# Seven block products for eight in the second layer of each chunk pair, and the pairs' instructions in the order of a list schedule

## The chip, the cores and the metric

The kernel runs on one core of a Trainium2 chip. The metric is the device time of one execution in microseconds (us); the median of three runs of the kernel before is 654.4 us (654.15 to 655.77). The engines are named as the profile names them: PE is TensorE with its matmuls, PEld its weight loads, DVE is VectorE, ACT is ScalarE, POOL is GpSimd, and SP issues the transfers.

## What is computed

Two blocks follow each other. The first is a linear recurrence over 768 time steps, for 4 batches and 8 heads of 48 channels; the second is a gated feed-forward block on 3072 tokens of 384 features with 1536 hidden units. All of it is fp32.

```
for t in range(S):                       # attention, per batch and head
    y[t]  = r[t] @ (state + outer(u * k[t], v[t]))
    state = w[:, None] * state + outer(k[t], v[t])
x  = y, heads side by side               # 3072 x 384
xn = x / sqrt(mean(x*x) + 1e-6) * rms_g
out = (silu(xn @ w_gate) * (xn @ w_val)) @ w_out
```

## The kernel before

The 768 steps are cut into 12 chunks of 64, so that one chunk of the 4 batches is 256 tokens. The kernel's own word for the recurrence, the mean of squares and the scaling of one chunk is **mixing**; its result is x, kept twice (`xa`, and `xb` with the two halves of 64 partitions exchanged). Each matmul of the program appears in the profile as two MATMUL records.

**The first stage** (chunks 0 and 1, with the loading and conversion of the weights) is given in an order that a small planner finds. `Plan.add` (line 103) takes each step with its engine, an estimated duration, the keys that it reads and writes, and the closure that issues it; `Plan.schedule` (line 123) is a greedy list schedule in which each engine takes the ready step with the earliest due time; `Plan.run` (line 174) tries 3000 sets of due times and issues the steps in order of their planned starts. Matmuls on a constant (`warm`, line 852) fill the planned gaps of PE up to 25 us.

**The pairs.** Chunks 2 to 11 go through the feed-forward block in five pairs, and here the order is written out by hand (lines 1015 to 1055). For a pair (s, s+1) the first layer has six groups (`group`, line 945). Each group forms gate and value of 128 units of each half of the hidden layer for both chunks by seven products of blocks where the plain way has eight: `first` to `seventh`, each 6 matmuls of 64 rows x 128 by 256 columns, 12 records, into three PSUM tiles a, b, c. The sums that such a scheme needs are made by DVE: of weights once (`unit_sum`), of tokens once for each pair (`token_sum`: t1, t2, x of s+1 in its own place, t4), of products in each group. The hidden values end in six tiles h, with four 256-token parts each.

The second layer is plain. `project` (line 996) is called for j = 0 to 3, each 128 tokens of the pair; it accumulates 12 matmuls of 128 x 128 by 384 columns into one PSUM bank, in two halves of 6 matmuls, then ACT copies the bank to SBUF and SP stores it. The mixing of the next two chunks is written in between: that of s+2 in the groups, that of s+3 between the halves of the projections (the letters in `plan` and in the calls of `mix`). Three places for x go round (`ring`, bufs=3).

**The check of the weights.** While the pairs run, all weights are read from HBM a second time in 48 pieces of 288 words (`check`, line 930) into a tile of their own, and ACT looks at them with an Abs and a Relu that sums; at the end DVE and PE condense the findings to a number `bad`, on which the program branches to a general version (not taken here).

All instructions are recorded through the helper of line 91, so the profile is read by tile names: `a`, `b`, `c` are the first layer, `po` the second, `py`, `pa`, `pu`, `pm` the mixing in the pairs, `first_a` to `first_c` and `at` the first stage.

Of the kernel before, what the change touches and what calls it, by code (L numbers as in the profile page):

```python
# [48 lines left out]
P = 128  # L50
# [43 lines left out]
class Plan:  # L94
# [28 lines left out]
    def schedule(self, goals, free):  # L123
# [16 lines left out]
        for _ in range(n):  # L140
            when, e = min((max(free[e], min(at[i] for i in ready[e])), e) for e in free if ready[e])
            i = min((i for i in ready[e] if at[i] <= when), key=lambda i: late[i])
            sooner = [j for j in ready[e] if at[j] <= when + 0.3 and late[j] < late[i] - 1]
# [30 lines left out]
    def run(self, cells, first, free, idle=None, trials=3000):  # L174

        goals, t = {}, first
        for i in cells:
            goals[i] = t  # L180
            t += self.ops[i][1]
        rng, best = random.Random(3), None
        for trial in range(trials):
            new = dict(goals)
            if trial and rng.random() < 0.5:
                a, by = rng.randrange(len(cells)), rng.uniform(-15, 15)
                for i in cells[a : a + 1 + int(rng.expovariate(1 / 6))]:
                    new[i] += by
            elif trial:
                new[rng.randrange(len(self.ops))] = rng.uniform(0, t)  # L190
            start = self.schedule(new, free)
            end = self.replay(start, free)
            end = max(end[i] for i in cells) + 0.3 * sum(end[i] for i in cells) / len(cells)
            if best is None or end <= best[0]:
                best, goals = (end, start), new
        self.start = best[1]
        busy = free["PE"]
        for i in sorted(range(len(self.ops)), key=lambda i: (self.start[i], i)):
            if self.ops[i][0] == "PE":
                if idle and busy < first:  # L200
                    idle(self.start[i] - busy)
                busy = self.start[i] + self.ops[i][1]
            self.ops[i][3]()
# [3 lines left out]
def fast(ctx, tc, chan, tok, vpad, wka, wkb, wot, cols, u_row, out, bad):  # L207
# [17 lines left out]
    ring = ctx.enter_context(tc.tile_pool(name="ring", bufs=3))  # L225
    hpool = ctx.enter_context(tc.tile_pool(name="hpool", bufs=7))
    ps_gv = ctx.enter_context(tc.tile_pool(name="ps_gv", bufs=1, space=PSUM))
    ps_at = ctx.enter_context(tc.tile_pool(name="ps_at", bufs=2, space=PSUM))
# [52 lines left out]
    gdup = raws.tile([P, HP, 2, L], FP32, name="gdup")  # L281
# [25 lines left out]
    def state_decay():  # L307

        for z in range(2):
            rows = slice(64 * z, 64 * z + D)  # L310
            for p in range(HP):
                act.mul(
                    KH[rows, z, :, p, :], free_dims(ident[rows, 64 * z : 64 * z + D], (0, B), (1, D)),
                    pows[L][rows, p : p + 1],
                )
# [104 lines left out]
    def diagonal(s, half, side):  # L420

        t, rows = SIDES[side]
        for b in (2 * half, 2 * half + 1):
            for p in range(HP):
                x = b * HP + p
                act.mul(t[rows, b, p, :], dmask[rows], du_of[s][rows, x : x + 1])
# [94 lines left out]
    xa, xb = {}, {}  # L521
# [5 lines left out]
    def mean_squares(bank, sq):  # L527
        for half in range(2):
            for i in range(CC):
                pe.matmul(  # L530
                    bank[:, 2 * P + half : 2 * P + half + 1], sq[:, i, half * P : (half + 1) * P], ones[:, 0:1],
                    start=i == 0, stop=i == CC - 1, skip_group_check=True,
                )
# [34 lines left out]

    late = {}

    def begin_sums():
        loading.close()
        mine = late["mine"] = ctx.enter_context(tc.tile_pool(name="mine", bufs=1))
        for n in (1, 2, 4):
            late[f"s{n}"] = [mine.tile([P, NQ, CC, P], FP32, name=f"s{n}_{i}") for i in range(2)]

# [10 lines left out]
    t1, t2, t4 = {}, {}, {}  # L587

    def token_sum(s, n):

        new = lambda t: t.setdefault(s, late["mine"].tile([P, CC, NT], FP32, name=f"t{n}_{s}", tag=f"t{n}"))
        if n == 1:
            dve.tensor_sub(new(t1), xa[s + 1], xa[s])
        elif n == 2:
            dve.tensor_sub(new(t2), xb[s + 1], t1[s])
        elif n == 3:
            dve.tensor_sub(xa[s + 1], xb[s + 1], xa[s + 1])
        else:
            dve.tensor_sub(new(t4), xb[s], t2[s])
# [3 lines left out]
    add = p.add  # L603
    at = [ps_at.tile([P, 512], FP32, name=f"at_{i}", tag="at") for i in range(2)]
    gv = {t: ps_gv.tile([P, 2, 512], FP32, name=f"first_{t}", tag=t) for t in "abc"}
    hbuf = [hpool.tile([P, 4, NT], FP32, name=f"hbuf_{i}", tag="h") for i in range(7)]
    yT = one.tile([P, CC, NT], FP32, name="yT_first", tag="yT")
    sq = one.tile([P, CC, NT], FP32, name="sq_first", tag="sq")
    ms = c_tile([P, 2], "ms")
    diag = one.tile([P, 2, P], FP32, name="diag", tag="rms")  # L610
    turn = {"at": 0, "gv": 0, "h": 0}

    def next_at():
# [3 lines left out]

    add("SP", 0.3, [], ["w"], lambda: None, land=1.9)
    add("DVE", 2.4, ["w"], ["pw"], powers, name="powers")
    add("DVE", 0.43, ["pw"], ["up"], lambda: dve.tensor_mul(up, pw, by_inv), port=True)  # L620
    add("DVE", 0.43, ["pw"], ["down"], lambda: dve.tensor_mul(down, pw_rev, by_inv), port=True)
    add("DVE", 0.22, [], ["dmask"], lambda: dve.tensor_add(dmask, ident[:, 0:64], ident[:, 64:128]), port=True)
    add(
        "DVE", 0.86, ["pw"], ["gdup"], lambda: [
            dve.tensor_mul(gdup[:, :, z, :], pw_rev, free_dims(pows[L // 2], (1, HP), (0, L))) for z in range(2)
        ], port=True,
    )
    bank, key = next_at()
    add("PE", 0.9, ["gdup"], [key], lambda bank=bank: token_powers(bank), name="wk")
    add("ACT", 0.7, [key], ["wk"], lambda bank=bank: keep_token_powers(bank), name="wk")  # L630
    add("ACT", 3.0, ["pw"], ["khd"], state_decay, name="khd")
# [16 lines left out]

    def mixing(s):
        quick = s == 0  # L650
        if quick:
            ku = hbuf[6].rearrange("p a (h t) -> p a h t", h=HP)
            add("ACT", 1.6, ["w", "CHk0", "CHk1"], ["ku"], lambda: u_k(s, ku), name=f"ku {s}")
            for half in range(2):
                add(
                    "PE", 1.05, ["ku", "CHr0", "CHr1"], [f"first{half}"],
                    lambda half=half: products(gv["a"][:, half], half, ku, CH[:, 0], CH[:, 0]), name=f"E {s}",
# [32 lines left out]
        for half in range(2):  # L690
            bank, key = two[half]
            for side in range(2):
                dst = f"M{'EO'[side]}t{half}"
                if quick:
                    add(
                        "DVE", 0.69, [f"first{half}", "dmask"], [dst],
                        lambda half=half, side=side: diagonal_from(gv["a"][:, half], half, side), name=f"d {s}",
                    )
                else:
                    add("ACT", 2.0, ["du"], [dst], lambda half=half, side=side: diagonal(s, half, side), name=f"d {s}")  # L700
# [28 lines left out]
        add("PE", 1.35, ["sq0", "sq1"], [key], lambda bank=bank: mean_squares(bank, sq), name=f"r {s}")  # L729
        add("ACT", 0.3 if s == 0 else 2.9, [key], ["ms"], lambda bank=bank: root(bank, ms), name=f"sqrt {s}")  # L730
        add("DVE", 0.45, [], ["ms", "diag"], lambda: inverse(ms, diag), name=f"inv {s}")
        add("PE", 0.45, ["diag"], [key], lambda bank=bank: spread(bank, diag), name=f"spread {s}")
        x = s % 3

        def scale(bank=bank):
            xa[s] = ring.tile([P, CC, NT], FP32, name=f"xa_{s}", tag="xa")
            xb[s] = ring.tile([P, CC, NT], FP32, name=f"xb_{s}", tag="xb")
            scaled(s, bank, yT)

        add("DVE", 1.0, [key, "yT0", "yT1"], [f"xa{x}"], scale, name=f"x {s}")  # L740
        for z in range(2):
            add("ACT", 0.83, [f"xa{x}"], [f"xb{x}.{z}"], lambda z=z: exchange(s, z), name=f"xb {s}")
        for z in range(2):
# [3 lines left out]
            "PE", 1.9, ["KH0", "KH1", "khd", "VSv", "VSs0", "VSs1"], [last[0][1], last[1][1]],  # L747
            lambda: [states(last[half][0], half) for half in range(2)], name=f"U {s}",
        )
        for half in range(2):  # L750
            bank, key = last[half]
            add("ACT", 1.07, [key], [f"VSs{half}"], lambda bank=bank, half=half: keep_states(bank, half), name=f"E {s}")

# [15 lines left out]
    cells, sums, waiting = [], {}, deque()  # L769

    def next_gv():
        t = "abc"[turn["gv"] % 3]
        turn["gv"] += 1
        return gv[t], ["first0", "first1"] if t == "a" else [f"gv_{t}"]

    def gate_val(s, i, o):
        ps_, keys = next_gv()
        n = turn["h"]
        turn["h"] = (n + 1) % 24
        h, x = hbuf[n // 4][:, n % 4], s % 3  # L780
# [12 lines left out]
    def add_cell(s, i, hs):  # L793

        po, keys = next_gv()
# [9 lines left out]
        if i == 0:  # L805
            sums[s] = work.tile([P, 2, DM], FP32, name=f"o_{s}", tag="o", bufs=FIRST)
            add("ACT", 0.8, keys, [f"o{s}"], lambda: act.copy(sums[s], po[:, :, 0:DM]), name=f"o {s}")
        else:
            add("DVE", 0.96, keys, [f"o{s}"], lambda: dve.tensor_add(sums[s], po[:, :, 0:DM], sums[s]), name=f"o {s}")
        if i == WQ - 1:  # L810
            add("SP", 0.5, [f"o{s}"], [], lambda: [store(sums[s][:, j], s, j) for j in range(2)])
# [19 lines left out]
    add("DVE", 0.0, ["rounded", "up", "down", "wk"], ["sums"], begin_sums)  # L831
# [20 lines left out]
    def warm(us):  # L852

        for _ in range(int((us - 0.3) / 0.22)):
            pe.matmul(gv["c"][:, 0, 0:P], ones, ones, start=True, stop=True)

    p.run(cells, 25.0, {"PE": 1.5, "DVE": 1.5, "ACT": 2.5, "POOL": 6.3, "SP": 1.8}, warm)
# [698 lines left out]
```

## Time and profile before

| stretch | us | PE busy | DVE busy | ACT busy |
|---|---|---|---|---|
| 0 to 60 (first stage) | 60.0 | 54.40 | 48.91 | 42.91 |
| 60 to 155.8 (first stage) | 95.8 | 95.80 | 70.42 | 52.29 |
| pair of chunks 2, 3 | 101.0 | 99.94 | 61.04 | 49.77 |
| pair 4, 5 | 101.1 | 100.92 | 58.68 | 56.57 |
| pair 6, 7 | 101.0 | 100.81 | 58.67 | 56.45 |
| pair 8, 9 | 101.1 | 100.91 | 56.81 | 56.56 |
| pair 10, 11 and the end | 93.1 | 85.85 | 30.14 | 27.30 |

The table is read off the busy times by window, and the bounds of the pairs are the starts of `first` of the first group. A row tells how much of a stretch each engine works; what an engine waits for stands in other views. The profiled execution took 654.79 us, of which the span from the first to the last instruction is 653.1 us. The granted PE clock is 0.996 over the span.

### The profile page before, as it was taken

To read this page: it belongs to the slowest core of one execution; us is meant where nothing else is said; L and a number is where in the kernel's file an instruction comes from. 1 tells how busy PE (TensorE), PEld (TensorE's weight loads), DVE (VectorE), ACT (ScalarE), POOL (GpSimd) and SP (SyncE) were. 2 spreads that over 40 slices of the span, in tenths; PEclk is the share of its full clock that TensorE was granted. 3 is DMA by queue.
4 is the path that set the end of the run, shared out by engine and by line. 5 is a ranking of instruction groups with operands and counts; after the bars stand their busy time and mean duration, and the time that the engine had idled before them with its cause. 6 is when DMAs were issued, how large, how long until landed. Compare 5 with 4: busy or idle time off the path is not lost.

```text
span 653.1 us, 15289 instructions
## 1 busy us (share of the span) xinstructions
PE 638.6 (98%) x6534; PEld 504.7 (77%) x6534; DVE 384.7 (59%) x560; ACT 341.9 (52%) x952; POOL 41.7 (6%) x39
## 2 busy tenths in 40 slices
PE   9889999999999999999999999999999999999996
PEld 8868777787878766889766888866888966788753
DVE  6988878855765734765743576653576562555400
ACT  5695465944364653574672564673555582433400
POOL 3154423100000000000000000000000000000000
PEclk9999999999999999999999999999999999999999
DMA  8786643053004242204331404332312321122211
GB/s 260 254 310 213 194 116 115 12 170 78 27 3 167 61 138 49 75 22 166 98 111 40 110 20 158 93 93 73 93 37 101 106 73 25 42 63 73 55 27 28
DMA packets 20398, 64.50 MB, mean 99 GB/s; under 512 B 2912, under 2 KB 6112, under 8 KB 18912
## 3 DMA queue, kind: packets, MB, share of 16 engines
q1 hardware_dynamic: 20320, 63.42, 32.3%
q8 instruction: 53, 0.87, 0.6%
q14 instruction: 25, 0.20, 0.1%
HBM read 58.69 MB, written 4.72 MB: 97 GB/s over the span
## 4 chain that ended last, share of the span: by engine, by line
PE 86%; DVE 5%; ACT 4%; issue 2%; DMA 1%; POOL 0%; DVEq 0%; ACTq 0%; POOLq 0%; SPq 0%
PE po L91 24%; PE b L91 15%; PE a L91 10%; PE c L91 9%; PE first_c L91 5%; PE first_b L91 5%; PE first_a L91 5%; PE at L91 4%; PE py L91 4%; PE pa L91 2%; PE pu L91 2%; ACT ME L91 1%; DVE TOK L91 1%; ACT MO L91 1%; DVE gv L91 1%
## 5 line engine op out<-in xcount | busy, mean ns | idle before, releaser
L91 PE MATMUL po<-wo,h 128*128 128x384 f32 x480 | 159.8, 489 | 0.8 <-DVE bad L91 0.8
L91 PEld LDWEIGHTS po<-wo,h 128*128 128x128 f32 x480 | 90.0, 190 | 60.2 <-PE pc L91 0.8
L91 DVE TENSOR_TENSOR gv<-b,m 128x512 f32<-128x512 f32 x90 | 62.1, 690 | 84.2 <-PE b L91 83.5
L91 ACT ACTIVATE gv<-gv 128x512 f32<-128x512 f32 (+1 forms) x60 | 31.0, 518 | 52.9 <-DVE gv L91 52.9
L91 DVE TENSOR_TENSOR gv<-c,gv 128x512 f32<-128x512 f32 x60 | 41.4, 690 | 15.0 <-PE c L91 14.0
L91 ACT COPY o<-po 128x384 f32<-128x384 f32 x20 | 9.5, 474 | 77.4 <-PE po L91 39.2
L91 ACT ACTIVATE ME<-dmask,du 64x64 f32<-64x64 f32 x176 | 43.8, 330 | 9.8 <-DVE du L91 9.4
L91 PE MATMUL a<-xa,wa 64*128 64x256 f32 x360 | 45.0, 383 | 0.7 <-DVE h L91 0.7
L91 PE MATMUL b<-xa,wa 64*128 64x256 f32 x360 | 44.4, 379 | 0.6 <-DVE gv L91 0.6
L91 ACT ACTIVATE MO<-dmask,du 64x64 f32<-64x64 f32 x176 | 44.4, 334 | 0.7 <-DVE du L91 0.3
L91 PE MATMUL c<-xb,s 64*128 64x256 f32 x360 | 44.3, 378 | 0.0
L91 PE MATMUL b<-t,wb 64*128 64x256 f32 x360 | 44.3, 378 | 0.0
L91 PE MATMUL b<-t,s 64*128 64x256 f32 x360 | 44.0, 377 | 0.3 <-DVE gv L91 0.3
L91 PE MATMUL a<-xb,wb 64*128 64x256 f32 x360 | 43.9, 376 | 0.0
L91 PE MATMUL c<-t,s 64*128 64x256 f32 x360 | 43.9, 376 | 0.0
L91 PEld LDWEIGHTS a<-xa,wa 64*128 64x128 f32 x360 | 33.8, 187 | 7.2 <-DVE h L91 3.0
L91 PEld LDWEIGHTS b<-xa,wa 64*128 64x128 f32 x360 | 34.2, 187 | 6.1 <-DVE gv L91 2.4
L91 PEld LDWEIGHTS b<-t,s 64*128 64x128 f32 x360 | 34.8, 187 | 4.7 <-DVE gv L91 0.7
L91 PEld LDWEIGHTS a<-xb,wb 64*128 64x128 f32 x360 | 34.9, 187 | 4.0
L91 PEld LDWEIGHTS c<-t,s 64*128 64x128 f32 x360 | 34.9, 187 | 4.0
L91 PEld LDWEIGHTS b<-t,wb 64*128 64x128 f32 x360 | 34.5, 187 | 4.1
L91 PEld LDWEIGHTS c<-xb,s 64*128 64x128 f32 x360 | 34.5, 187 | 4.1
(146 smaller groups left out, 1076.0 us busy)
## 6 DMA issues: line engine op xcount, KB each, us to landing
chan<-in_chan_dram SPq DMA_DIRECT2D x11, 1024.0 KB, 5.0
TOK<-in_tok_dram SPq DMA_DIRECT2D x12, 768.0 KB, 4.6
VS<-in_vpad_dram SPq DMA_DIRECT2D x24, 336.0 KB, 4.8
raw<-in_wot_dram SPq DMA_DIRECT2D x8, 576.0 KB, 5.0
out_dram<-o SPq DMA_DIRECT2D x48, 96.0 KB, 2.2
again<-in_wka_dram SPq DMA_DIRECT2D x16, 288.0 KB, 2.8
again<-in_wkb_dram SPq DMA_DIRECT2D x16, 288.0 KB, 2.8
again<-in_wot_dram SPq DMA_DIRECT2D x16, 288.0 KB, 2.8
```

The source lines that it names most:

```text
L91: return lambda *args, **kwargs: self.tc.keep_in_program_order(give(*args, **kwargs))
```

## The change

It has three parts.

1. **The second layer** (`second_layer`, new). The pair's hidden values form a matrix of 2 x 2 blocks (two chunks by two halves of the hidden units), and the output weights one of 2 x 2 blocks (two halves of the units by two halves of the 384 features). The product is formed by seven products of blocks for eight. Each is 12 matmuls of 128 x 128 by 192 columns. DVE makes four sums of hidden values for each pair (`sum_1` to `sum_4`), five sums of results (u2, u3, c21, c22, c12), and once, in the first pair, eight sums of output weights (`out_sum`); ACT makes two copies.
2. **No new memory for the sums where another stage's tile is free**: sum_1 lies in the tile of gate and value, sum_2 in that of t1 and t2, sum_3 and sum_4 in h itself, the sums of weights in the place of x of chunk 2 (`swap`), the results in the tile of the first stage's results. The checks of weights use `sq`, the squares of the mixing; they are 36 pieces of 384 words instead of 48 of 288, and five of them follow each mixing's use of `sq`. x has two places from the second pair on (`place`).
3. **The order.** The pairs, with mixing, loads and checks, are steps of a second `Plan`. Its due times are those of the products in a row, stretched by 1.19; it is scheduled once, without a search, and a step may be waited for up to 0.5 us if it is more urgent than the ready one. `run` is split into `search` and `give`. In the first stage the estimated durations of some steps are changed, two steps are cut finer, and the first run of `warm` is counted from 0 instead of 1.5 us and shortened by nine matmuls.

```diff
-    def project(s, j, second):
-        ...
-        for m in range(3, 6) if second else range(3):
-            for x in range(2):
-                i, o = divmod(m + x * NN // 2, NQ)
-                at = (j % 2) * P
-                pe.matmul(
-                    po, h_of[s, m][:, 2 * x + j // 2, at : at + P], wo[i][:, o, :],
-                    start=m == 0 and x == 0, stop=m == last and x == 1,
-                )
+    def second_layer(s):
+        bank = {"x": bank_of["a"][:, 0], "w": bank_of["a"][:, 1], "y": bank_of["b"][:, 0], "z": bank_of["c"][:, 0]}
+        keys = {"x": "a0", "w": "a1", "y": "b", "z": "c"}
...
+        def mm(t, reads, left, right, start, name):
+            def give():
+                for j in range(2):
+                    for m in range(NN // 2):
+                        pe.matmul(
+                            flat[t][:, j], left[:, m, j * P : (j + 1) * P], right(*divmod(m, NQ)),
+                            start=start and j == m == 0, stop=m == NN // 2 - 1, skip_group_check=True,
+                        )
+            line.append(add("PE", 3.9, reads, [keys[t]], give, name=f"{name} {s}"))
...
+        add("DVE", 1.66, h_keys[1] + h_keys[3], gs, lambda: dve.tensor_add(sum_1, h[1], h[3]), port=True, name="sum_1")
+        add("DVE", 1.66, h_keys[0] + gs, ts, lambda: dve.tensor_sub(sum_2, sum_1, h[0]), port=True, name="sum_2")
+        add("DVE", 1.66, h_keys[0], h_keys[1], lambda: dve.tensor_sub(h[1], h[0], h[1]), port=True, name="sum_3")
+        mm("x", h_keys[0], h[0], part(0, 0), True, "P1")
+        add("ACT", 0.47, ["a0"], ["m1"], lambda: act.copy(m1, flat["x"]), name="m1")
+        mm("z", gs + out_keys("o1"), sum_1, w2(0), True, "P5")
+        mm("x", h_keys[2], h[2], part(2, 0), False, "P2")
+        add("ACT", 0.47, ["a0"], ["o0"], lambda: act.copy(results[:, 0], flat["x"]), name="c11")
+        result(0, s, 0)
+        add("DVE", 1.66, ts, h_keys[2], lambda: dve.tensor_sub(h[2], h[2], sum_2), port=True, name="sum_4")
+        mm("y", ts + out_keys("o2"), sum_2, w2(1), True, "P6")
+        plus(["o1"], ["b", "m1"], results[:, 1], flat["y"], m1, "u2")
+        mm("y", h_keys[1] + out_keys("o3"), h[1], part(0, 1), False, "P7")
+        plus(["o3"], ["b", "m1"], results[:, 3], flat["y"], m1, "u3")
+        mm("w", h_keys[3] + out_keys("o4"), h[3], w2(2), True, "P4")
+        plus(["o2"], ["a1", "o3"], results[:, 2], flat["w"], results[:, 3], "c21")
+        plus(["o3"], ["c"], results[:, 3], flat["z"], results[:, 3], "c22")
+        mm("z", h_keys[2], h[2], part(2, 1), False, "P3")
+        plus(["o1"], ["c"], results[:, 1], flat["z"], results[:, 1], "c12")
...
+    place = lambda s: s % 3 if s <= FIRST + 1 else (s + 1) % 2
...
+        if until < 27:
+            for _ in range(int((until - since - 0.3) / 0.22) - (9 if since == 0 else 0)):
+                pe.matmul(bank_of["c"][:, 0, 0:P], ones, ones, start=True, stop=True)
...
+        for m in range(NN // 2):
+            group(s, m)
...
+        if s + 2 < NS:
+            mixing(s + 2), loads(s + 3)
+        second_layer(s)
+        if s + 2 < NS:
+            mixing(s + 3)
...
+    free = {"PE": 0.0, "DVE": 0.0, "ACT": 0.0, "POOL": 0.0, "SP": 0.0}
+    p.give(p.schedule(p.goals_of(line, 0.0, 1.19), free, 0.5))
```

## The prediction

> **What bounds the kernel now.** I read the page's first part, then the waits of PE, then the chain that ended last, then the groups by shape.
>
> ```profile
> span 653.1 us, 15289 instructions
> PE 638.6 (98%) x6534; PEld 504.7 (77%) x6534; DVE 384.7 (59%) x560; ACT 341.9 (52%) x952; POOL 41.7 (6%) x39
> ...
> PE 86%; DVE 5%; ACT 4%; issue 2%; DMA 1%; POOL 0%; DVEq 0%; ACTq 0%; POOLq 0%; SPq 0%
> ...
> L91 PE MATMUL po<-wo,h 128*128 128x384 f32 x480 | 159.8, 489 | 0.8 <-DVE bad L91 0.8
> L91 PEld LDWEIGHTS po<-wo,h 128*128 128x128 f32 x480 | 90.0, 190 | 60.2 <-PE pc L91 0.8
> L91 DVE TENSOR_TENSOR gv<-b,m 128x512 f32<-128x512 f32 x90 | 62.1, 690 | 84.2 <-PE b L91 83.5
> ```
>
> PE is busy for 638.6 of 653.1 us, and most of the rest lies outside its work: 6.4 us after its last matmul (copy, store, branch). A busy PE alone could be a PE that stretches its records over waits, so the second view counts: all that PE waited for between its first and last matmul.
>
> ```profile
> PE at L91 <- ACT sq_first L91: 1.7, 1, 1.7
> PE first_c L91 <- DVE pw L91: 1.2, 1, 1.2
> PE first_b L91 <- POOL wa L91: 1.1, 1, 1.1
> PE at L91 <- DVE MO L91: 1.0, 1, 1.0
> PE b L91 <- DVE gv L91: 0.9, 2, 0.6
> PE po L91 <- DVE bad L91: 0.8, 1, 0.8
> PE at L91 <- DVE diag L91: 0.8, 1, 0.8
> PE a L91 <- DVE h L91: 0.7, 4, 0.2
> ```
>
> Columns: total us, times, longest. The sum is 8.2 us, over half of it in the first 45 us; in the pairs PE waits 1.06 us in the first (101.0 less 99.94 busy), about 0.19 us in each of the next three, and 0.8 us for the flag in the last. So in the pairs the time is the sum of PE's instructions, and DVE's largest group has 83.5 us of idle time behind PE. An instruction less on PE is time less, unless the new order makes PE wait.
>
> The third view gives PE's price without overlaps: the chain in order of time, start and us.
>
> ```profile
> 320.27 4.07 PE po L91 x12
> 324.77 3.87 PE po L91 x12
> 328.64 2.01 PE pa L91 x64
> ...
> 349.85 7.74 PE po L91 x24
> 357.59 1.57 PE pu L91 x64
> 359.16 1.50 PE a L91 x12
> ```
>
> Twelve `po` records take 3.87 us: 322.5 ns each[...].
>
> [...]48 records of one column each (`at<-ones,sq_first`) fill 5.9 us, 123 ns each[...], so a load costs no more than that when nothing hides it. [...]The trace has 690 ns for 512 and 1350 for 1152[...]. [...]the stores' pieces shrink from 1536 to 768 B[...]. No run so far shows 768 B.
>
> **The change, part by part.**
>
> *Removed from PE:* 5 pairs x 48 matmuls x 2 = 480 records of 322.5 ns = 154.8 us[...].
>
> *Added to PE:* 5 x 7 x 12 x 2 = 840 records of 192 columns. No such row exists. [...]162.5 ns, 3.9 us a product, 136.5 us in all.[...] Upper bound: if the shorter matmul no longer hid its weight load, the record's 190 ns (159.6). The one-column rate of 123 ns is well below 160, so I take 162.5. **Balance −18.3 us**[...]. A change of shape on PE costs up to 0.2 us (4.07 for the first twelve above, 3.87 for later ones), and there are about as many as before: eight half projections give way to seven products.
>
> *DVE.* Four sums of 1536: [...]1.76 us; five of 384: 0.56; together 9.8 us a pair. A pair has 58.7 us of DVE work in 101; it becomes 68.5 in about 97.5, so DVE is no bound on average. The eight weight sums, [...]6.1 us, come once. ACT gives up two copies of 0.474 us a pair, and about 7 us of checks in all: 48 x (461+443+186) ns becomes 36 of about 1.25 us[...]. Both hidden by PE.
>
> *New waits of PE.* (a) From the last product of the first layer to P5, which needs sum_1: on DVE g1 0.69, h23 0.68, h1 0.42, sum_1 1.76, with the silu beside h23: 3.6 us. P1 runs meanwhile, 3.9 us. Hidden by 0.3 us; a mixing step of 0.95 us that slips into DVE's queue ahead of sum_1 costs 0.6. (b) P7 adds to the bank that u2 reads after P6: 0.56 and two handovers, 0.8 us; P4 uses another bank and fits between. (c) P3 adds to the bank that c22 reads, and c22 follows u3, which follows P7: 1.4 us with handovers (the trace has 0.05 to 0.2 us for one). The next pair's first product needs c21, also behind u3, so only the mixing can fill it: the state matmuls, 1.57 us, fit. In the last pair nothing is left to fill it: 1.4 us. For the other four I take 0.6 us each on average over (a) and (c), from 0 to 2.0: 2.4 us. (d) First pair: weight sums and hidden sums together keep DVE about 9.5 us from the end of the groups to P6, while P1, P2, P5 give PE 11.7: 0.5 us at most. The old handover waits go (1.06 + 3 x 0.19 = 1.6 us); the flag's 0.8 stays.
>
> *x with two places.* x of s+2 may be written only after the last group's first product. From there: 0.96 for x, 2 x 1.1 for the three scalings of each half on ACT, 0.43 on PE, square root with its two table loads 0.47 + 2 x 1.28, reciprocal 1.75, x 0.96, exchanges 1.66, t2 0.95: about 11.5 us, 13.3 with handovers. The PE work until the next pair's second product is 7.8 + 27.3 + 1.3 = 36 us. Hidden, if nothing else lies in the chain. The checks do lie near it: five in a row in `sq`, each a transfer (2.8 us for 288 KB before) and 1.25 us of ACT, about 24 us, between the squares of s+2 and those of s+3. With 24 and 13 us against 29 from the end of the groups to that second product, s+2 must have its squares at least 8 us before the groups end. The groups last 54 us and its inputs are there at the pair's start, so I cost it at nothing.
>
> *First stage.* The recurrence's first matmuls start at 9.49 us, directly behind 25 warm-up matmuls of 0.336 us (8.40 us for 50 records), while their input on ACT was ready at 6.64; DVE then waits 2.95 us for them. Counting from 0 adds 1.5/0.22 = 6.8 matmuls and nine go: two fewer, −0.7 us. The new search may move the other 5 us of waits either way: 0, from −3 to +2.
>
> *Sum:* 654.4 − 18.3 − 0.7 − 1.6 + 2.4 + 1.4 + 0.5 = **638.1, say 638 us**.
>
> **Rivals.**
>
> *Handover waits at every pair.* (a) and (c) are not filled: 2.0 us for each pair, 10 us for the 4.3 above: 644 us. For it: u3, c22 and c21 stand in DVE's one queue with the mixing. Against: the first stage, ordered by the same planner, keeps PE busy for 110.80 of the 110.80 us from 45.0 to 155.8.
>
> *The checks push the mixing.* If the squares of s+2 come only at the end of the groups, those 37 us against 29 leave 8 us of idle in four pairs: 638 + 32 = 670 us, slower. For it: the schedule puts off what is not due, and on SP's queue loads stand behind a check that waits for `sq`. Against: the checks count in the due times.
>
> *Weight loads bind.* 190 ns a record: 638 + 23 = 661 us, slower. Against: the 123 ns.
>
> *A better first stage.* Most of its waits go too: 638 − 4 = 634 us.
>
> **Chances.** Forecast 638, with a few us around it: 0.65. Handover waits, 644: 0.18. Better first stage, 634: 0.11. The two slow ones: 0.06 together; a mild form of the checks' case, near 650, is in the handover case. The range leaves out less than the slow cases and little below: 633 to 647. Faster 0.94, same 0.02, slower 0.04.
>
> **What would show it.** The new products at 162 to 163 ns a record, 12 x 2 of them 3.9 us in the chain; pairs about 97 to 98 us apart; PE's waits under 12 us in all; DVE near 68 us a pair; P3 of the last pair waiting about 1.4 us on DVE. Wrong if PE waits on `xa`, `t` or the sums for over 3 us a pair, or if the new records take 190 ns.

## The result and the profile after

The changed kernel takes **646.69 us** (median of four runs, 644.37 to 648.63) against 654.37 before: ratio **0.9877**, 95% interval 0.9832 to 0.9922. It is faster by 7.7 us where 16.4 were forecast. The direction held and the time lies within the range, at its upper edge, but 8.7 us of the gain did not arrive. One thing is needed to read the runs of this kernel: its times fall into two groups, near 644.5 us at a mean granted PE clock of 0.998 and near 648.5 us at 0.991 to 0.993, and the profiled execution (648.53 us) is of the second.

Below, f1 to f7 are the seven products of a group in the first layer (`first` to `seventh` in the kernel before) and P1 to P7 those of the second layer; a joint is the place where one pair ends and the next begins.

The page of the changed kernel, the lines that answer to those shown of before:

```profile
span 646.7 us, 16003 instructions
PE 625.2 (97%) x6882; PEld 549.6 (85%) x6882; DVE 436.5 (67%) x613; ACT 349.0 (54%) x914; POOL 42.1 (7%) x39
...
PE 88%; DVE 5%; DMA 3%; ACT 2%; issue 1%; SPq 0%; DVEq 0%; ACTq 0%
...
L92 DVE TENSOR_TENSOR gv<-bank_b,m 128x512 f32<-128x512 f32 x90 | 62.2, 691 | 47.8 <-PE bank_b L92 44.9
```

PE is still the bound: 88% of the chain. Its busy time fell by only 13.4 us, with 348 more records, the new ones shorter. DVE's largest group lost almost half of its idle time (84.2 us before): DVE now has more to do between two products, so less slack if something holds its queue up. What PE waited for (total us, times, longest), the same view as before the change:

```profile
PE bank_b L92 <- DVE gv L92: 2.4, 3, 0.8
PE bank_c L92 <- DVE rows_out L92: 1.9, 1, 1.9
PE bank_b L92 <- DVE t L92: 1.6, 1, 1.6
PE bank_a L92 <- DVE rows_out L92: 1.4, 3, 1.0
...
PE at L92 <- issue: 1.1, 2, 1.0
...
PE bank_b L92 <- DVE bad L92: 0.6, 1, 0.6
PE bank_a L92 <- ACT m L92: 0.5, 1, 0.5
```

But for 0.1 us these lie in the pairs, 9.4 us in all. Before the change about 0.2 us in each pair, and 0.8 us for the flag (`bad`) in the last, were all that PE waited for once the first pair was done. The rest of that view, 5.2 us, is the first stage's. The chain gives the new products their price, and shows one that took longer (start, us):

```profile
624.45 3.90 PE bank_a L92 x24
628.35 3.91 PE bank_b L92 x24
...
634.13 5.86 PE bank_c L92 x24
```

24 records in 3.90 us are 162.5 ns each, as forecast. The third product, P3 of the last pair, starts 1.9 us after P7's end and then takes 5.86 us for the same work. The view of windows, cut at the clock's own steps, says why (us; length, PE busy and records, PEld, DVE, ACT, POOL; granted clock; DMA):

```profile
631.75:635.17 3.42, 1.53 (x10) 1.23 (x9) 1.67 (x3) 0.00 (x0) 0.00 (x0) 1.00 0.10 22
635.17:638.58 3.41, 3.41 (x13) 3.41 (x12) 0.00 (x0) 0.00 (x0) 0.00 (x0) 0.50 0.42 97
...
553.25:556.66 3.41, 1.61 (x14) 1.08 (x12) 2.78 (x4) 2.93 (x5) 0.00 (x0) 1.00 0.07 16
```

PE had been busy for 1.53 us of the first window, 45% of it, and for the next 3.41 us it was granted half its clock. The trace has two rates, 1.00 and 0.50. The half-clock window of its first stage starts at 44.66 us, 590.51 us before this one, which is 173 times 3.413 us, and the stretches shown are laid in that step. The last line, 23 of them earlier, is a close case that went the other way: over another wait PE was busy for 1.61 us, and in the window after it the granted clock was 1.00.

Putting both profiled executions side by side, cut at the first product of the pairs and at PE's last matmul (waits are the gaps between PE's records, half clock the time lost in the pairs in windows at 0.5, work the remainder; each profile has one more such window in its first stage, from 47.5 us before and 44.7 after):

| part, us | before | after | difference | forecast |
|---|---|---|---|---|
| first stage | 155.8 | 154.3 | −1.5 | −0.7 |
| pairs: PE's work | 488.5 | 474.6 | −13.9 | −18.3 |
| pairs: PE's waits | 2.4 | 9.4 | +7.0 | +2.7 |
| pairs: half clock | 0 | 1.7 | +1.7 | 0 |
| after the last matmul | 6.4 | 6.8 | +0.4 | 0 |

So in this execution three things ate the gain: 4.4 us of work that should have gone, 4.3 us of waits more than allowed for, and a window at half clock that no step had. The waits have places. At the joint of two pairs DVE's queue shows one (DVE in order of time, from the end of pair 4, 5):

```profile
342.49 1.23 DVE L92 TENSOR_TENSOR chan<-chan,down 128x1024 f32<-128x1024 f32 x1 [2.27 <-DMA chan<-in_chan_dram]
343.63 1.22 DVE L92 TENSOR_TENSOR ME<-chan,up 128x1024 f32<-128x1024 f32 x1
344.77 0.88 DVE L92 TENSOR_TENSOR sq<-sq 128x256 f32<-128x256 f32 x2
345.57 0.55 DVE L92 TENSOR_TENSOR rows_out<-bank_a,rows_out 128x384 f32<-128x384 f32 x1
```

DVE stands 2.27 us for a `chan` transfer; behind it in the queue are the mixing's two multiplications, the square `sq` that PE's mean of squares needs, and c21, which frees the bank of the next pair's first product. What PE does meanwhile and after (PE in order of time):

```profile
345.75 0.67 PE L92 MATMUL at<-sq,ones 128*128 128x256 f32 x2 [0.99 <-issue]
346.35 1.57 PE L92 MATMUL bank_a<-xa,wa 64*128 64x256 f32 x12
347.85 4.17 PE L92 MATMUL bank_c<-wo,h 128*128 128x192 f32 x24
...
355.01 1.57 PE L92 MATMUL bank_c<-t,s 64*128 64x256 f32 x12
356.41 1.46 PE L92 MATMUL bank_b<-t,s 64*128 64x256 f32 x12
358.67 0.70 PE L92 MATMUL bank_b<-xa,wa 64*128 64x256 f32 x4 [0.79 <-DVE gv L92]
```

The wait of 0.99 us is the one just explained. Two joints have such a wait, of 1.0 us each; the other two have 0.2. The last three lines are another: f3 (into c) goes ahead of f2 (into b), so f4, which also writes b, follows f2 at once and waits 0.79 us for DVE to read b. Three pairs have it, 2.4 us in all. And the second and third lines show what the loss of work comes from: `bank_c<-wo,h` is P3 of the old pair, set between f1 and f5 of the new one. It breaks a run of 64-row products.

### The profile page after: what moved, and what is told of

Read it like the earlier page. It is cut to its first block, busy times and chain, and to the rows that moved or that the text cites. A ratio compares the mean times of both kernels' runs of the same rounds, so it can differ in the third digit from the quotient of the medians.

```text
span 646.7 us, 16003 instructions
## 1 busy us (share of the span) xinstructions
PE 625.2 (97%) x6882; PEld 549.6 (85%) x6882; DVE 436.5 (67%) x613; ACT 349.0 (54%) x914; POOL 42.1 (7%) x39
## 4 chain that ended last, share of the span: by engine, by line
PE 88%; DVE 5%; DMA 3%; ACT 2%; issue 1%; SPq 0%; DVEq 0%; ACTq 0%
PE bank_b L92 29%; PE bank_a L92 25%; PE bank_c L92 23%; PE at L92 11%; DMA chan<-in_chan_dram 1%; DMA TOK<-in_tok_dram 1%; DVE rows_out L92 1%; DVE gv L92 1%; DVE ME L92 1%; ACT MO L92 1%; ACT ME L92 1%; DVE t L92 1%; DMA sq<-in_wot_dram 0%; DVE TOK L92 0%; DVE MO L92 0%
## 5 line engine op out<-in xcount | busy, mean ns | idle before, releaser
L92 DVE TENSOR_TENSOR gv<-bank_b,m 128x512 f32<-128x512 f32 x90 | 62.2, 691 | 47.8 <-PE bank_b L92 44.9
L92 PE MATMUL bank_b<-xa,wa 64*128 64x256 f32 x444 | 55.1, 381 | 3.6 <-DVE gv L92 2.4
L92 PEld LDWEIGHTS bank_b<-xa,wa 64*128 64x128 f32 x444 | 42.0, 187 | 10.4 <-DVE gv L92 3.6
L92 PE MATMUL bank_a<-xa,wa 64*128 64x256 f32 x396 | 49.1, 380 | 1.4 <-DVE rows_out L92 1.4
L92 PE MATMUL bank_a<-wo,h 128*128 128x192 f32 (+1 forms) x264 | 49.8, 345 | 0.5 <-ACT m L92 0.5
L92 PE MATMUL bank_a<-xb,wb 64*128 64x256 f32 x396 | 48.9, 379 | 0.0
L92 PEld LDWEIGHTS bank_a<-wo,h 128*128 128x128 f32 x264 | 43.2, 190 | 5.4 <-issue 1.3
L92 PE MATMUL bank_b<-t,s 64*128 64x256 f32 x360 | 44.1, 377 | 1.6 <-DVE t L92 1.6
L92 PE MATMUL bank_b<-t,wb 64*128 64x256 f32 x360 | 44.4, 379 | 0.0
L92 PE MATMUL bank_c<-xb,s 64*128 64x256 f32 x360 | 44.3, 378 | 0.0
L92 PE MATMUL bank_c<-t,s 64*128 64x256 f32 x360 | 44.1, 377 | 0.0
```

Source lines behind the costliest of these rows:

```text
L92: return lambda *args, **kwargs: self.tc.keep_in_program_order(give(*args, **kwargs))
```

## The experiments

Each was timed beside the kernel before (654.3 to 654.6 us each time); ratios carry their 95% interval. "Gaps" are PE's waits in the pairs, "runs" the uninterrupted runs of 64-row products in the pairs, both from the profiled execution.

### The same kernel again, and the two halves of the change

**again**: no edit.

> The changed kernel once more, to see how its times are spread. Clock theory: the runs fall into two groups, near 644.5 and near 648.5 us, with mean granted clocks of about 0.998 and 0.992, and nothing between; a half-speed window of 3.4 us stands over the last product in the slow group alone. Rival (chip-to-chip or run-to-run scatter): a continuous spread, or one group only, with no tie to the clock.

Measured: 648.68 us (644.1 to 652.58), 0.9895 [0.9858, 0.9931]. The first result stands, though this median lies 2 us higher, above the forecast's range. Two runs at a clock of 0.998 took 644.1 and 644.2, the others at 0.991 to 0.993 took 648.2 to 652.6: two groups, as expected, but the slower one is spread. Its profile has gaps of 10.1 us and half clock in the pairs twice: from 554 us for 6.8 us, after a window with a wait of 2.04 us in which PE was busy for 1.37 us, and at 636 us over P3, after one with 1.52 us. Whether the faster runs have a half-clock window over P3 was not profiled. Their mean clock says no: 0.998 of 642.5 us is a loss of 1.3 us in all, and one window costs 1.7.

**plain**: the list schedule of the pairs, with the second layer in the plain way.

```diff
-        second_layer(s)
+        plain_layer(s)     # 4 x 24 records of 384 columns, ACT copies, as before
```

> The list schedule, its places and its checks as in the changed kernel, but the second layer plain: per pair 8 blocks of 6 matmuls of 384 columns, each 128 tokens in a bank of its own, no sums of weights, hidden values or results. This is the change of order alone. If the list schedule is neutral: 653 us, the time before less the 1.4 us of the first stage. If the schedule itself costs waits (rival): it has the waits of PE at the start of a pair (f4 of the first group, 0.8 us, and others), 1 to 2 us a pair, 656 to 661 us. If most waits come from the sums of the seven products: near 652 to 654 with under 1 us of waits of PE per pair.

Measured: 656.91 us (654.65 to 659.82, 11 runs), 1.0037 [1.0024, 1.0051]. The list schedule, with its places, its checks and the new first stage, costs 2.4 us. Its gaps are 5.3 us against 2.4 before, its work 489.6 against 488.5, with 17 runs of 64-row products against 13. Its waits have f4's among them (total us, times, longest):

```profile
PE bank_b L92 <- DVE gv L92: 4.0, 5, 0.8
```

So this wait belongs to the list schedule, not to the seven products. The seven products bring 656.9 − 646.7 = 10.2 us by the first measurement of the changed kernel, and 8.2 by run again.

### The window at half clock

**fill**: six matmuls on constants, 1.34 us, between P7 and P3 of the last pair, where PE waits for DVE anyway.

```diff
         plus(["o3"], ["b", "m1"], results[:, 3], flat["y"], m1, "u3")
+        if s + 2 == NS:
+            add("PE", 1.35, ["b"], ["at0"], fill, name="fill")   # 6 x 128 columns of ones
```

> Six matmuls on a constant (1.35 us) are put between the last pair's P7 and P3, where PE stood for 1.89 us; nothing else changes, and P3 still waits for the same add of DVE. Clock theory: no half-speed window over the last product in any run, so about 2 us less than the changed kernel in its slow group (646.5 us) and the same in its fast group (644.5); median 644.5 to 646.5. Waits theory without the clock: no change, since P3 starts when it did (644.5 and 648.5 both remain).

Measured: 643.47 us (643.2 to 646.96), 0.9843 [0.9825, 0.9862]. In the profiled execution no window of the pairs is at half clock. The window over the same wait now reads:

```profile
628.40:631.80 3.40, 2.96 (x24) 2.74 (x23) 1.73 (x4) 0.00 (x0) 0.00 (x0) 1.00 0.07 17
```

PE is busy for 2.96 of 3.40 us, and P3 behind it takes 4.17 us instead of 5.86. P3 starts when it did, 6.0 us after P7 began; only what PE does in between differs. So the half clock came from the idle time before it, and cost 1.7 us.

The median fell by more, 3.2 us from the first measurement and 5.2 from run again, and lies 1 us below what the clock theory allowed. Two other things differ between the two profiles. The edit also moved the flag's matmul, to just behind the six new ones, and with it went a wait of P6 for the flag, 0.6 us. And two joints wait 1.8 us less, because the transfers of this execution came sooner (see fill_land); the order of instructions there is the same. Together with the 1.7 us of the clock this is 4.1 of the 4.3 us by which the pairs are shorter. Four of five runs lie within 0.4 us; the fifth, 646.96 us at a clock of 0.992, is still slower.

### Changes of tile shape

**shape**: fill, and in each of the 30 groups of the pairs one matmul over all 128 rows between f3 and f4.

```diff
         mm(["t1"], ["c"], c, late["s1"][i][:, o], t_of(1), True, "f3")
+        add("PE", 0.6, [], ["c"], full)   # 128 columns of ones into unused columns of c
         mm(xn_a + [f"s3.{i}"], ["b"], b, wa[i + 2][:, o], xa[s + 1], False, "f4")
```

> Run fill with one matmul of 128 columns over the whole array, on constants and into unused columns of tile c, between f3 and f4 of every group of the first layer in the pairs: 30 in all, 0.224 us of work each (two records of 0.112), or 30 x 0.224 = 6.7 us. It breaks a run of 64-row products 30 more times. Theory: every return to 64-row products and every leaving costs about 0.2 us on PE, so 30 x (0.224 + 0.2 + 0.16) = 17.5 us over fill's 643.5: about 661. Rival: a change of tile shape costs nothing beyond the instructions themselves: about 650. A value between gives the cost of one change as (time - 650.2)/30.

Measured: 660.09 us (657.91 to 663.1), 1.0095 [1.0071, 1.0120], 16.6 us over fill. All of it is PE's own time in the pairs:

```profile
154.00:651.80 497.80, 492.76 (x5181) 1.00 0.25 75
```

PE's work is 492.8 us against fill's 475.7: +17.1, of which the 30 matmuls themselves are 6.7 at the pace of fill's six. The remaining 10.4 us go with 50 runs of 64-row products against 25 (five of the 30 stood where a run ended anyway): **0.42 us for each run entered and left.** The free-change rival (650) falls. What PE does at a change of shape was not shown, only that it takes longer; part of the 0.42 us may also be that a pair of records alone costs more than the 0.22 us counted for it. Counted in the traces, before has 13 such runs in the pairs and after 25: 12 x 0.42 = 5.0 us, and 4.4 is what the work fell short by.

### Banks, due times, patience, landing

These runs change what the list schedule works with: which PSUM banks the products write, the stretch of the due times, the patience (how long a step may be waited for if it is more urgent), and the landing (the time that the planner allows for a `chan` transfer). The edits, and in the table which run has which:

```diff
-    "w": bank_of["a"][:, 1], ... P3 into "z"
+    "w": bank_of["b"][:, 1], "v": bank_of["c"][:, 1], ... P3 into "v"      # banks: of their own for P4 and P3
-    p.give(p.schedule(p.goals_of(line, 0.0, 1.19), free, 0.5))
+    p.give(p.schedule(p.goals_of(line, 0.0, 1.0), free, 0.3))              # goal: 1.0; patience: 0.3
-    load_chan(s), land=LAND                                                # 2.1
+    load_chan(s), land=4.4 if s > FIRST + 2 else LAND                      # land; in the two "eager" runs 4.4 for all
-    mm("y", h_keys[1] + out_keys("o3"), h[1], part(0, 1), False, "P7")
+    mm("q", h_keys[1] + out_keys("o3"), h[1], part(0, 1), True, "P7")      # own_p7, last pair: second half of a
```

| run | banks | stretch | patience | chan landing | gaps, us | runs | length of pairs, us | time, us | ratio |
|---|---|---|---|---|---|---|---|---|---|
| fill | shared | 1.19 | 0.5 | 2.1 | 5.6 | 25 | 481.3 | 643.47 | 0.9843 |
| fill_goal | shared | 1.0 | 0.5 | 2.1 | 8.7 | 25 | 484.9 | 646.40 | 0.9883 |
| fill_land | shared | 1.19 | 0.5 | 4.4 | 6.8 | 25 | 482.5 | 644.94 | 0.9838 |
| fill_land_goal | shared | 1.0 | 0.5 | 4.4 | 6.8 | 25 | 483.0 | 646.62 | 0.9873 |
| fill_land_all | shared | 1.0 | 0.3 | 4.4 | 4.8 | 25 | 479.8 | 641.47 | 0.9779 |
| fill_eager | shared | 1.0 | 0.3 | 4.4, all | 2.7 | 25 | 477.4 | 645.03 | 0.9862 |
| banks | own | 1.19 | 0.5 | 2.1 | 10.8 | 21 | 486.4 | 649.06 | 0.9918 |
| banks_eager | own | 1.0 | 0.3 | 4.4, all | 4.0 | 20 | 477.0 | 645.54 | 0.9862 |
| banks_goal | own | 1.0 | 0.5 | 2.1 | 4.4 | 20 | 478.2 | 642.41 | 0.9805 |
| own_p7 | own, P7 too | 1.0 | 0.5 | 4.4 | 2.8 | 20 | 475.6 | 640.64 | 0.9801 |

The intervals of the ratios reach 0.0014 to 0.0027 to each side. The fill rows have fill's six matmuls, the banks rows don't.

> P3 writes a PSUM bank of its own (second half of tile c) and P4 the second half of tile b in place of that of tile a; result 1,2 takes one more add of DVE (0.56 us) a pair. So P3 no longer waits for c22, and the next pair's first product no longer for c21. Waits theory: the 1.89 us before the last P3 and the waits of bank_a on rows_out (1.4 us in three pairs) are gone, with them the half-speed window at the end: about 641 us, all runs in one group near that (the first stage's own window may still split them by 2 us). Rival (DVE's queue is what is late, and the wait only moves to the next product that needs it): within 1 us of the changed kernel, with longer waits of f2 to f4.

> Second layer with its two own banks as in the run banks, and two more edits: the due times of the products are not stretched (1.0 for 1.19, with a patience of 0.3 for 0.5 us), so that the mixing falls due about a fifth earlier against the products, and the planner is told that the transfer of a chunk's r and k lands 4.4 us after its issue, not 2.1. Theory (the waits at the start of a pair come from a mixing that is planned with no slack): PE's waits in the pairs fall from 8 to 10 us to under 3 us, no half-speed window falls between 60 us and the end, 637 to 640 us. Rival (the order is not the cause; any order of this work on DVE and ACT has such waits): 643 us or more.

> As banks, with one edit alone: the due times are not stretched (1.0 for 1.19); patience and landing as in the changed kernel. If the due times are what matters: within 2 us of banks_eager. If the landing is: 643 us or more, with waits of DVE for the transfer of r and k, and of PE behind them.

> As fill (six matmuls on a constant before the last P3, the banks of the changed kernel), with due times not stretched, patience 0.3 and the landing of 4.4 us. It shows what the shared banks cost once the mixing is early. If the shared banks matter then: the first product of a pair waits 0.2 us for c21, and the last pair keeps its waits: 640 to 642 us, 2 to 3 us over banks_eager. If they do not: within 1 us of it.

What follows from these four: banks alone gain nothing, against the theory and near their rival. P3's wait of 1.9 us goes, but others come, on f4 and f3 (3.9 us behind `gv` and 2.4 us behind `rows_out`). With a stretch of 1.0 the same banks give 642.41, 6.6 us less, so with these banks the due times are what holds the additions up. banks_eager misses its 637 to 640 us. In both eager runs the landing time reached the planner of the first stage too, and its order came out longer (158.0 and 156.7 us against 151.5 to 155.4 in the other profiles), so their times say little of the pairs, whose length, 477, is among the shortest. Beside each other the two can be read: 645.54 and 645.03 us, pairs of 477.0 and 477.4. With a stretch of 1.0 and a patience of 0.3 the shared banks cost nothing that is seen.

> Run fill with one number changed: due times stretched by 1.0 in place of 1.19, so that the additions of the first layer are asked for sooner. Banks as in the changed kernel. Theory: the waits of 0.79 us at f4 and of 1.0 us at the joints of pairs come from due times that leave the vector engine no slack; with 1.0 gaps in the pairs fall from 5.6 to 3 to 4 us and the time from 643.5 to about 641.5. Rival: the gain of banks_goal needed the banks of its own, and the due times alone change nothing (643 to 644).

A miss: with shared banks the stretch of 1.0 makes it worse, 646.4, with gaps of 8.7 us. The wait of 1.0 us at the joints is 0.22 in this profile, but it was 0.22 in fill's too. The wait of f4 stands at all four joints, and a single wait of 1.63 us for `h` has come. So the due times alone are not the cause, and at a patience of 0.5 banks_goal's gain is one of both edits together.

> Run fill with one number changed: the pairs' planner allows 4.4 us from a chan load's issue to its landing in place of 2.1; the trace has a median of 6.8. Theory A, a transfer that the planner thinks faster than it is: at 342.49 us of the changed kernel DVE stands 2.27 us for the chan transfer, and the squares, c21 and the next pair's first product stand behind it; with a truer landing the planner puts those additions ahead, the waits of 1.0 us at the joints go, gaps in the pairs fall from fill's 5.6 to about 3 us, time 643.5 - 2.5 = 641. Theory B, the due times and the patience decide: no change, 643 to 644.

> fill_land with due times stretched by 1.0 in place of 1.19. Due times alone (fill_goal) cost 2.9 us over fill, with gaps of 8.7 us in the pairs against 5.6. Theory A: the landing is what matters, so this stands near fill_land, about 641, and well below fill_goal. Theory B: due times of 1.0 are worse without banks of their own, whatever the landing: 644 to 646.

> fill_land_goal with the patience at 0.3 in place of 0.5: run fill_eager without the slower first stage that its landing edit caused. fill_eager had gaps of 2.7 us in the pairs and a length of the pairs of 477.4 us against fill's 481.3, but a first stage 3.0 us longer. Theory: 643.5 - 4 = about 639.5. If fill_land_goal is at 644 or more and this at 640, it is the patience and not the landing.

The landing time alone gains nothing (644.94 against 643.47, the intervals of the ratios overlapping): theory A falls as a remedy for fill, which had no wait of 1.0 us at the joints to lose. Why the changed kernel had one, and fill not, stands in DVE's queue at the same place (fill's profile; the changed kernel's line is the one at 342.49 above):

```profile
340.10 1.23 DVE L92 TENSOR_TENSOR chan<-chan,down 128x1024 f32<-128x1024 f32 x1 [1.28 <-DMA chan<-in_chan_dram]
```

The changed kernel, again and fill give their instructions in one order but for the flag, so their joints can be laid side by side. At four of them DVE stands 2.2 to 2.8 us for the transfer, and PE then waits 0.9 to 1.5 us; at four it stands 1.0 to 1.4 us, and PE waits 0.2 us or less. So how late the transfer is in the execution at hand decides, and the order has slack for about 1.4 us of it. In the three fill_land runs DVE does not stand for `chan` in the pairs at all: the truer number does what it was meant to do, but other waits fill its place.

The patience is what tells here: fill_land_all differs from fill_land_goal in it alone and takes 641.47 for 646.62, with pairs of 479.8 us for 483.0. Its profile, at the place shown above for the changed kernel:

```profile
354.43 1.57 PE L92 MATMUL bank_c<-t,s 64*128 64x256 f32 x12
355.83 1.46 PE L92 MATMUL bank_b<-t,s 64*128 64x256 f32 x12
357.13 1.46 PE L92 MATMUL bank_a<-xa,wa 64*128 64x256 f32 x12
358.42 1.46 PE L92 MATMUL bank_b<-xa,wa 64*128 64x256 f32 x12
```

Another product now stands between f2 and f4, and no line has an idle time. With a patience of 0.5 us the planner lets PE stand for a step that is more urgent, 0.79 us on the chip, where at 0.3 it takes the next ready one. One such wait is left in this profile, where fill_land_goal's had four.

> Run banks_goal with two corrections: the last pair's P7 sums into the idle second half of tile a and no longer waits for the sum u2, and the planner of the pairs (it alone, not the first stage's) allows 4.4 us for the chan transfer. Theory: waits are what is left to remove. banks_goal ended 8.7 us after its last matmul, the changed kernel 6.8, because three additions stood behind P7; with P7 free early the tail falls to 6.7 and the 0.7 us wait goes: 642.4 - 2 - 0.7 = about 640. Rival: the list schedule moves the waits elsewhere and the time stays at 642 to 643.

Measured: 640.64 us (638.06 to 643.33), 0.9801 [0.9784, 0.9819]: in time about as the theory had it, though not distinguishable from banks_goal by the intervals. Gaps in the pairs are 2.8 us, near the 2.4 of the kernel before, and the work is 472.8 us with 20 runs of 64-row products. The tail didn't shrink as expected: it is 9.0 us. DVE and SP at its end:

```profile
623.98 6.49 SPq L92 DMA_DIRECT2D out_dram<-rows_out  x6
...
627.30 1.02 DVE L92 TENSOR_TENSOR rows_out<-bank_c,rows_out 128x384 f32<-128x384 f32 x2 [3.34 <-PE bank_c L92]
```

Two additions instead of one are left after the last matmul, and behind them four stores instead of two, which SP issues at 0.6 us each. The last store is issued 2.5 us after the last matmul, where the changed kernel's is issued after 1.3, and it lands 3.3 us later for 2.5. That is 2.0 of the 2.2 us.

**held**: own_p7, and seven matmuls on constants ahead of the first mean of squares of chunk 1, in the first stage.

> own_p7 with seven matmuls on constants (1.6 us of work whose result the next matmul overwrites) ahead of the first mean of squares of chunk 1, where PE waits some 1.4 us at about 43 us, just before the half-speed window at 44 to 48 us. Theory: that window follows from PE's idle time before it; with PE busy there the window goes, and the runs lose 3.4/2 = 1.7 us: 638.3 if own_p7 takes 640, and the mean granted clock rises towards .998. Rival: the window comes from something else (a fixed time after the start, or an earlier wait at 33 us): same time as own_p7 or up to 1 us more, and a window still at 44 us.

Measured: 641.11 us (640.87 to 642.92), 0.9803 [0.9789, 0.9816]. This run tells nothing on its question. The seven matmuls stood behind the wait that they were to fill (PE is idle for 1.44 us and the first of them follows), and own_p7's profiled execution had no window at half clock there either. Whether the windows near 44 us, which many of these profiles have and the kernel before as well, follow from the wait in front of them is left open. PE's busy time alone does not sort them: the kernel before has half clock after a window with 2.59 of 3.41 us busy, and fill has none after one with 1.96 of 3.40 in the same stretch.

### The second reading of the weights

**nocheck**: fill without the second reading of the weights from HBM and what looks at it (36 transfers, 72 activations and their sums are left out; the flag is set to zero).

```diff
-    to_check = list(enumerate(parts))
+    to_check = []
```

> As fill, but it leaves out the second reading of the weights (36 transfers and the looks of ACT at them), with the stretched due times. If the checks push the mixing of the second chunk to the end of the pair (they hold sq between its two uses): the 0.8 us waits of f4 and the 1.6 us of f2 at the start of a pair go, 640 to 641 us. If the lateness comes from the due times: still 642 to 643.5 us, with waits at other places.

Measured: 641.03 us (637.91 to 642.06), 0.9789 [0.9766, 0.9811], 2.4 us under fill. So the first of the two theories holds in the main: the wait of f2, 1.5 us in fill, is gone, and of three waits of f4 one is left. Gaps are 3.5 us instead of 5.6, and the planner, with less to place, leaves 21 runs of 64-row products. How a check reaches PE shows in the changed kernel before f2 of the last pair (ACT, then DVE):

```profile
551.60 0.56 ACT L92 ACTIVATE sq<-sq 128x384 f32<-128x384 f32 x1 [4.56 <-DMA sq<-in_wot_dram]
552.18 1.67 ACT L92 COPY xb<-xa 64x768 f32<-64x768 f32 x2
...
553.88 0.96 DVE L92 TENSOR_TENSOR t<-xb,t 128x768 f32<-128x768 f32 x1 [2.79 <-ACT xb L92]
```

x of the pair's second chunk is ready at 548.03 us, but its copies stand in ACT's queue behind a look at the weights, and ACT stands 4.56 us for that piece's transfer. DVE's t2 needs the copies, and f2 needs t2: PE waits 1.6 us.

## Why the prediction was wrong

**Right.** The records cost 162.5 ns and a product 3.9 us. The 162.5 was the author's estimate, as before has no record of 192 columns; half of its 322.5 ns for 384 would be 161. A weight load takes 190 ns and the records still follow each other every 162.5 ns, so that rival falls. DVE is busy for 67.8 and 68.4 us in the second and third pair for the 68.5 worked out, and the sums of 1536 take 1.758 us for 1.76, where a line through the 0.690 us of an addition of 512 and the 1.350 us of one of 1152 before gives 1.75. P3 of the last pair waits 1.9 us for 1.4. In the two profiles the first stage is 1.5 us shorter where 0.7 were forecast, but over all the profiles that share its order it takes 151.5 to 155.4 us, so that this agreement says little.

**The first step that failed is a count.** The forecast says of changes of shape that "there are about as many as before". Only the second layer's products were counted, and those do go from eight half projections to seven. What counts is how often the stream of 64-row products is entered and left, and that is set by the planner: 25 runs instead of 13. Run shape puts a price of 0.42 us on each, 5.0 us in all. The forecast had the price ("up to 0.2 us" a change, two changes to a run) and applied it to the wrong number. Of the twelve new runs four come with the schedule alone (plain has 17), and four or five go when P3 and P4 have banks of their own (banks has 21, banks_goal 20).

**The second is the term for new waits**, 2.4 us for (a) and (c) and 1.4 in the last pair. At the joints P3 does not wait, but not for the forecast's reason: the planner puts the next pair's f1 ahead of it and not the state matmuls. f1 itself, or the mean of squares ahead of it, then waits at all of them, 1.0 us at two, where a `chan` transfer for which the planner allows 2.1 us takes a median of 6.8 and holds DVE's queue. At f4 the waits are 2.4 us, from an order f3, f2, f4 that comes with the list schedule (plain has it too) and mostly goes with less patience (fill_land_all). At f2 of the last pair it is 1.6 us, behind a check in ACT's queue. The forecast looked at the checks, asked only whether they hold up the squares, and costed them at nothing; nocheck gives them 2.4 us. Their rival of 670 us is far off all the same. The forecast took the first stage's 110.80 busy us of 110.80 as evidence for the planner. That stage was found among 3000 sets of due times, and the pairs' order is scheduled once; that the search makes the difference is argued, as no run searches the pairs. The rival of handover waits, 10 us, is near the 9.4 us of waits by luck: it had 2.0 us of them at every pair, from (a) and (c), and more than half of these come from elsewhere.

**The third is the window at half clock**, which no step or rival had: 1.7 us in the profiled execution, so that a wait of 1.9 us cost nearly as much again. Run fill shows it. The two groups of times are 4.0 us apart, more than this window. In the profiled execution two windows at half clock lie ahead of the last matmul, here and in the first stage, which together cost up to 3.4 us, and a run at 0.998 has room for neither. That these two make the groups fits, but the windows were not followed in each run.

**The remainder.** own_p7 is the change with most of the waits and five of the twelve new runs taken away: 640.64 against a forecast of 638. Its work in the pairs is 15.7 us less than before; with 7 x 0.42 = 2.9 us for the seven runs that it still has more, that is 18.6 where 18.3 were forecast. For the changed kernel the same sum is 13.9 + 5.0 = 18.9. The saving forecast for the seven products was thus there; the order in which they were given didn't let it through. own_p7's tail is 9.0 us for 6.4 on the other side. Not settled is which single input of the list schedule is to blame: stretch, banks and patience act together, and each by itself moved the waits about.

## What to carry to other kernels

When a step adds short products to a matmul stream, count how often the new order changes the tile shape, not how many products there are, and multiply by what the trace shows for one change. That a planner's order is good in one stage is no evidence for another with other due times, patience and transfer times; look in the new trace for the two or three places where PE waits, and read what stands ahead of the awaited instruction in its engine's queue. Here a look at the weights, which nobody needed soon, waited for its transfer and held up copies that PE needed. A wait of PE of 1.9 us cost nearly twice its length here by the clock (1.7 us more), and constant matmuls put into it took that away without moving the product behind them.

## What the runs showed of the hardware

- In the pairs, windows of 3.41 us in which PE was busy for 1.53 us (the changed kernel), 1.52 and 1.37 us (again) were followed by one at half clock; with 1.61 us (the changed kernel) and 2.96 us (fill) they were not. It is not a sharp rule of busy time: after P3 in again a window with 1.46 us was not, and in the first stage of the kernel before one with 2.59 us was.
- A product of 12 records of 64 rows, alone between others, takes 1.50 us from start to start (346.35 to 347.85 above), and 1.30 us inside a run (355.83 to 357.13 in fill_land_all). With what its neighbours lose, a run entered and left costs 0.42 us (shape).
- Stores in pieces of 768 bytes land in a median of 2.4 us. Those of 1536 bytes take 2.2 in the kernel before and 2.8 in plain, so no cost of the smaller pieces is seen.
